# Layer one's mixing takes its block product P2 as seven inner products, placed last, and the sums for them are made earlier

## The chip, the cores and the metric

The kernel runs on one core of one Trainium2 chip. The metric is the device time of one execution in microseconds. Engines: PE (matmuls, with its weight loads PEld), DVE (vector), ACT (scalar), POOL (GpSimd) and SP, which here only issues DMAs. Each engine works through its own instructions in the order in which the program lists them. An instruction that waits holds up all that stand behind it on its engine, and the same holds for the DMAs that one queue issues.

The code counts layers from 0: `L == 0` is the first pair of blocks, which the title's "layer one" means. From here on it is called **layer zero**, and the second pair **layer one**, as in the code.

## What is computed

Four residual blocks in a row on x (2048 tokens by 512 features), A B A B:

```python
def _B_ref(x, w_in, w_sp, b_sp, w_out):
    z = _gelu(jnp.einsum("bsd,df->bsf", x, w_in))
    z1 = z[..., :Fh]
    z2 = _layernorm(z[..., Fh:], axis=-1)
    g = jnp.einsum("ts,bsf->btf", w_sp, z2) + b_sp[None, :, None]
    return jnp.einsum("bsf,fd->bsd", z1 * g, w_out)
...
x = x + _A_ref(_layernorm(x, axis=-1), A_wqkv, A_wo)
x = x + _B_ref(_layernorm(x, axis=-1), B_w_in, B_w_sp, B_b_sp, B_w_out)
x = x + _A_ref(_layernorm(x, axis=-1), A_wqkv, A_wo)
x = x + _B_ref(_layernorm(x, axis=-1), B_w_in, B_w_sp, B_b_sp, B_w_out)
```

A is linear attention with 32 heads. In B, `w_in` is 512 by 1792 (Fh = 896), `w_sp` is 2048 by 2048 and mixes the tokens, `w_out` is 896 by 512. Both layers use the same weights.

## The kernel before, in words

Tokens lie in 16 tiles of 128. Every value that is multiplied is split into a high part (ACT copies it to the matmul's type, `high`, line 100) and a low part (DVE subtracts, `low`, line 103), and a product is three matmuls: high by high, high by low, low by high (`mm3`, line 113; `acc`, line 1355).

Each layer runs through four stages. *P1* is the attention's first half. *P2* (class at line 605, `run` at 915) is the **token stage**: steps s = 1 to 18, in which a tile goes through attention's second half, its layernorm, and both halves of `w_in`. It leaves z2 in the tiles `z0` to `z15`, and z1 in DRAM. *P4* (class at line 1129, `run` at 1466) is the **mixing** `w_sp @ z2`, followed by the **output stage** (16 steps `o(i)`, line 1446): z1 times g, by `w_out`, added to x.

**The mixing as seven products.** `w_sp` is taken as 2 by 2 blocks and z2 as two halves of tokens by two groups of features (H1 and H2, with H3 the 128 columns left over), so that seven block products, P1 to P7, stand for eight. Each has eight steps k. A step has 24 matmuls of 512 columns where it also does H3 (`WITH3`: six for `delta`, 18 for `beta`), else 18. The order is P4, P2, P1, P6, P7, P5, P3 (`ORDER`). Some products go on in the banks of the one before: P1 in P2's `delta` (layer zero only), P6 and P7 in P1's `beta`, P3 in P5's. After a product's last step `evac` (line 1387) adds its banks into `gb`, and units that are then complete are queued for `gates` (line 1372): one a step, z1 loaded in one step and multiplied in by POOL in the next.

**Block sums.** P6, P7, P5 and P3 take sums of blocks of `w_sp`. `Sums` (line 1008) makes them in layer zero and keeps them in DRAM for both layers: 64 additions of 128 by 512 on POOL, two to a tick (`tick`, line 1035). The ticks come with token steps 8 to 18 and mixing steps 1, 4, 7 and 8 on. A tick first stores what the last one made, and then fetches ahead.

**The inner seven.** In layer one, P2 is itself taken as seven products of half the size, `("N", d)`, d = 0 to 13, two steps for each (`nested_mm`, line 1283), 12 matmuls a step. They use two banks X and up to two banks Y. After each product's second step, `nested_mm` itself adds the banks into `gb` on DVE (lines 1313 to 1326). Their operands are built by `token_sums`, `nested_high` and `nested_low` (lines 1240 to 1281). Three of the products take blocks of `w_sp` as they are, and four take sums that `Inner` (line 1055) makes in 16 units: a DVE addition or subtraction, a high part on ACT, a low part on DVE, and stores to DRAM. Four units stand in layer zero's token stage, four in its output stage, eight in layer one's token stage.

**One step of the mixing**, g, in this order (`run`, lines 1480 to 1506): `prepare` splits the weight of step g+2 and the tile of step g+3 (line 1204); the matmuls of step g; the DMA for the weight of step g+4 (from SP, or from POOL's queue for an inner sum); a tick of `Sums`; `gates`; in P3's steps a piece of `w_out` (`wpiece`, line 1425; its parts take over the tags of z0 to z13) and, in the last one, `zsplit(0)`, which splits the first token tile for the output stage (line 1437); then `evac`:

```python
self.mm(g)
...
    if k == 7:
        self.zsplit(0)
if p != "N" and k == HT - 1:
    self.evac(p)
```

SBUF is held as 22 pages (128 by 512), six quads for weights and split tiles, and four bigs; PSUM has eight banks. A slot that is freed goes to the end of its list, and a new tile takes the first one of it, so it waits for the last reader of that slot.

Of the kernel before, what the change touches and what calls it, by code (L numbers as in the profile page):

```python
# [21 lines left out]
NF = FH // P  # L22
# [4 lines left out]
DEFER = 6  # L27

# [25 lines left out]
def mixer_kernel(ctx: ExitStack, tc: tile.TileContext, x_in, wqkv, wo_d, win1_d, win2_d, wsp_d, bsp_d, wout_d,  # L54
# [550 lines left out]
    class P2:  # L605
# [309 lines left out]
        def run(self, sums):  # L915
            w1 = self.win1
            for s in range(1, NT + 3):
# [28 lines left out]
                else:  # L946
# [51 lines left out]
                if s == 7:  # L998
                    sums.fetch()
                if s > 7:  # L1000
                    sums.tick()
# [6 lines left out]
    class Sums:  # L1008
# [3 lines left out]
        def __init__(self):  # L1012
            self.s = {(m, k): dram.tile([P, 2, 512], F32, name=f"s{m}_{k}") for m in range(1, 5) for k in range(HT)}
            self.todo = deque((k, j, h) for k in range(HT) for j in range(2) for h in range(2))
            self.ahead = deque(self.todo)
            self.raw, self.made, self.done = {}, [], []

        def fetch(self):
            if self.ahead:
                k, j, h = self.ahead.popleft()  # L1020
                at = ((j, k), (j, k + HT), (2 + j, k)) if h == 0 else ((2 + j, k + HT),)
                self.raw.setdefault((k, j), []).extend(load(wsp_d[n, s]) for n, s in at)

        def store(self):

            for m, k, j, t in self.made:
                nc.sync.dma_start(self.s[m, k][:, j, :], t)
            pages.put(*self.done)
            self.made, self.done = [], []

        def add(self, m, k, j, t, a, b):
            nc.gpsimd.tensor_tensor(t, a, b, op=OP.add)  # L1032
            self.made.append((m, k, j, t))

        def tick(self):
            self.store()
            if not self.todo:
                return
            if not self.raw:
                self.fetch()  # L1040
            self.fetch()
            k, j, h = self.todo.popleft()
            if h == 0:
                a21, a22, a11 = self.raw[k, j][:3]
                self.add(1, k, j, a22, a21, a22)
                self.add(3, k, j, a21, a21, a11)
                self.done = [a21]
            else:
                _, a22, a11, a12 = self.raw.pop((k, j))
                self.add(2, k, j, a11, a22, a11)  # L1050
                self.add(4, k, j, a12, a11, a12)
                self.done = [a22, a11, a12]


    class Inner:
# [3 lines left out]
        def __init__(self):  # L1059
# [3 lines left out]
            self.raw, self.open, self.parts = {}, None, []  # L1063

# [8 lines left out]
        def out(self):  # L1073
            for m, k, n, p in self.parts:
                nc.sync.dma_start(self.d[m][k // 2][:, k % 2, n, :], p.bitcast(F32))
                pages.put(p)
            self.parts = []

        def finish(self, late=False):
# [5 lines left out]
            l = pages.get(PAGE, F32R)  # L1085
# [8 lines left out]
        def unit(self, late=False):  # L1094
# [20 lines left out]
            h = pages.get(PAGE, F32R)  # L1115
# [6 lines left out]
        def begin(self, n):  # L1122

            self.fetch()
            self.fetch()
            self.due, self.left = 4 * n, 4 * n - 2


    class P4:
# [3 lines left out]
        ORDER = ("P4", "P2", "P1", "P6", "P7", "P5", "P3")  # L1133
        WITH3 = ("P4", "P2", "P1", "P5")
# [6 lines left out]
        def __init__(self, p2, sums):  # L1141
# [3 lines left out]
            self.nested = p2.seven  # L1145
            self.steps = []
            for p in self.ORDER:
                if p == "P2" and self.nested:
# [7 lines left out]
            self.wout = {}  # L1156

        def fetch(self, g):
# [12 lines left out]
            elif p in ("P1", "P2", "P4"):  # L1171
                n, s = {"P1": (2, k), "P2": (2, k + HT), "P4": (0, k + HT)}[p]
# [5 lines left out]
        def operand(self, g):  # L1178
# [4 lines left out]
            if p == "P2":  # L1183
                return b[:, 0:512], 1.0, None
# [98 lines left out]
        def nested_mm(self, g):  # L1283
# [24 lines left out]
            V, bs = nc.vector, self.bs  # L1308
            for i in range(2):
                u = {n: [self.unit(2, i), self.unit(2, 2 + i), self.unit(3, i), self.unit(3, 2 + i)][n - 1]  # L1310
                     for n in range(1, 5)}
                if name == "P1":
                    V.tensor_add(u[1], self.X[i], bs[2])
# [4 lines left out]
                elif name == "P7":  # L1318
                    V.tensor_add(u[4], self.X[i], bs[3])
# [268 lines left out]
```

## Time and profile before

| | |
|---|---|
| three timed runs | 1383.07, 1383.12, 1383.37 us (median 1383.12) |
| the profiled execution | 1383.13 us |
| its span, first to last instruction | 1381.4 us |
| granted PE clock | 1.00 in the whole span |
| layer zero: mixing, output stage | 350.0 to 622.0, 622.0 to 698.2 us |
| layer one: mixing, output stage | 1034.7 to 1301.2, 1301.2 to 1377 us |
| layer one: the inner seven | 1078.2 to 1116.3 us |
| HBM | 173.87 MB read, 80.48 MB written |

Rows of groups give line, engine, operation, what it writes and reads, count, busy time, mean ns of one, and idle time ahead with what ended it. Rows of a timeline give start, duration, engine, line, and in brackets the idle time ahead and what ended it. Rows of windows give, for each stretch, its length, then the busy time (count) of PE, PEld, DVE, ACT and POOL, the PE clock, the share of time that the DMA engines are busy, and GB/s. A matmul's duration runs from its start to the modelled end of its way through the array; the next one starts earlier.

### The profile page before, as it was taken

How to read it: one execution, taken by the hardware profiler on the slowest of the kernel's cores; microseconds unless marked ns; L12 is line 12 of the kernel's file. 1: busy time of each engine (PE TensorE's matmuls, PEld its weight loads, DVE VectorE, ACT ScalarE, POOL GpSimd, SP SyncE). 2: the span in 40 equal slices, each digit the busy share in tenths (PEclk: the TensorE clock that was granted, in tenths of full speed). 3: DMA queues.
4: the chain of work that ended last, by engine and by line, in shares of the span. 5: the costliest groups of instructions: out<-in, count | busy, mean ns of one | idle time of the engine just before them, and what ended most of it. 6: DMA issues, size and time to landing. Idle time of an engine off the chain costs nothing.

```text
span 1381.4 us, 17855 instructions
## 1 busy us (share of the span) xinstructions
PE 1374.9 (100%) x6209; PEld 1153.7 (84%) x6209; DVE 942.2 (68%) x1383; ACT 603.9 (44%) x944; POOL 444.1 (32%) x521
## 2 busy tenths in 40 slices
PE   9999999999999999999999999999999999999998
PEld 7888888888888888888888888888888888888887
DVE  7776887754755487677667768877768555775642
ACT  6674544334433234233357655544454432342410
POOL 3343454544145451432113434533220101133310
PEclk9999999999999999999999999999999999999999
DMA  5542367777768974466944414677365744444442
GB/s 176 169 130 62 115 191 229 252 232 257 243 234 293 284 246 131 144 228 219 354 128 153 137 54 130 207 228 248 128 203 177 267 154 133 169 134 155 168 147 91
DMA packets 158523, 255.54 MB, mean 185 GB/s; under 512 B 13408, under 2 KB 57312, under 8 KB 157408
## 3 DMA queue, kind: packets, MB, share of 16 engines
q1 hardware_dynamic: 153680, 239.59, 53.5%
q0 software_dynamic: 2880, 11.54, 2.6%
q10 hardware_dynamic: 1872, 3.28, 0.6%
q8 instruction: 48, 0.79, 0.2%
q14 instruction: 43, 0.35, 0.1%
HBM read 173.87 MB, written 80.48 MB: 184 GB/s over the span
## 4 chain that ended last, share of the span: by engine, by line
PE 100%; DVE 0%; ACT 0%; issue 0%; DVEq 0%
PE bank L117 19%; PE bank L116 19%; PE bank L115 19%; PE bank L1359 12%; PE bank L1357 12%; PE bank L1358 12%; PE bank L1302 1%; PE bank L1299 1%; PE bank L1301 1%; PE bank L830 1%; PE bank L829 1%; PE bank L828 1%; PE bank L253 1%; PE bank L441 0%; PE bank L472 0%; ACT pg L101 0%
## 5 line engine op out<-in xcount | busy, mean ns | idle before, releaser
L1359 PE MATMUL bank<-qd,pg 128*128 128x512 f32 x736 | 286.6, 389 | 0.0
L1357 PE MATMUL bank<-qd,pg 128*128 128x512 f32 x736 | 286.6, 389 | 0.0
L1358 PE MATMUL bank<-qd,pg 128*128 128x512 f32 x736 | 286.6, 389 | 0.0
L1223 DVE TENSOR_TENSOR qd<-qd,qd 128x1024 fp32r<-128x1024 f32 x110 | 152.1, 1383 | 122.0 <-ACT qd L1213 121.4
L1213 ACT ACTIVATE qd<-qd 128x1024 fp32r<-128x1024 f32 x110 | 116.5, 1059 | 230.9 <-DMA qd<-s 110.3
L1358 PEld LDWEIGHTS bank<-qd,pg 128*128 128x128 f32 x736 | 138.2, 188 | 28.9
L1359 PEld LDWEIGHTS bank<-qd,pg 128*128 128x128 f32 x736 | 138.2, 188 | 28.5
L1357 PEld LDWEIGHTS bank<-qd,pg 128*128 128x128 f32 x736 | 138.2, 188 | 28.5
L1379 POOL TENSOR_TENSOR bg<-bg,pg 128x512 f32<-128x512 f32 x56 | 82.5, 1477 | 236.1 <-DMA pg<-z 221.3
L117 PE MATMUL bank<-qd,pg 128*128 128x512 f32 x380 | 148.5, 391 | 0.0
L230 POOL TENSOR_SCALAR rs<-mv 128x1 f32<-128x1 f32 x95 | 40.0, 422 | 317.2 <-DVE mv L228 312.6
L1032 POOL TENSOR_TENSOR pg<-pg,pg 128x512 f32<-128x512 f32 x64 | 91.2, 1425 | 92.2 <-DMA pg<-in_wsp_dram 83.8
L241 ACT ACTIVATE pg<-pg,nb,rs 128x512 f32<-128x512 f32 x63 | 51.1, 811 | 149.1 <-POOL nb L235 136.6
L115 PE MATMUL bank<-qd,pg 128*128 128x512 f32 x284 | 110.8, 390 | 0.0
L116 PE MATMUL bank<-qd,pg 128*128 128x512 f32 x284 | 110.7, 390 | 0.0
L101 ACT ACTIVATE pg<-pg 128x512 fp32r<-128x512 f32 (+1 forms) x111 | 68.0, 617 | 91.4 <-DVE pg L292 40.7
L115 PE MATMUL bank<-bg,qd 128*128 128x448 f32 x256 | 94.1, 368 | 0.0
L116 PE MATMUL bank<-bg,qd 128*128 128x448 f32 x256 | 93.7, 366 | 0.0
L117 PE MATMUL bank<-bg,qd 128*128 128x448 f32 x256 | 93.5, 365 | 0.0
L104 DVE TENSOR_TENSOR pg<-pg,pg 128x512 fp32r<-128x512 f32 (+1 forms) x109 | 80.8, 744 | 14.2 <-ACT pg L101 13.6
L292 DVE STREAM_TRANSPOSE pg<-pg 128x512 f32<-128x512 f32 x79 | 85.3, 1080 | 5.1 <-DMA pg<-xt 2.4
L116 PE MATMUL bank<-wo,qd 128*128 128x512 f32 x224 | 87.2, 389 | 0.0
(186 smaller groups left out, 2845.5 us busy)
## 6 DMA issues: line engine op xcount, KB each, us to landing
qd<-s SPq DMA_DIRECT2D x64, 512.0 KB, 3.4
qd<-in_wsp_dram SPq DMA_DIRECT2D x46, 512.0 KB, 4.8
pg<-in_wsp_dram SPq DMA_DIRECT2D x80, 256.0 KB, 4.9
s<-pg SPq DMA_DIRECT2D x64, 256.0 KB, 5.2
pg<-x SPq DMA_DIRECT2D x64, 256.0 KB, 3.5
pg<-z SPq DMA_DIRECT2D x56, 256.0 KB, 3.7
x<-pg SPq DMA_DIRECT2D x48, 256.0 KB, 3.0
z<-pg SPq DMA_DIRECT2D x44, 256.0 KB, 2.6
```

Source lines behind the costliest of these rows:

```text
L104: nc.vector.tensor_sub(l, src, h.bitcast(F32))
L115: nc.tensor.matmul(out, ah, bh, start=start, stop=False)
L116: nc.tensor.matmul(out, ah, bl, start=False, stop=False)
L117: nc.tensor.matmul(out, al, bh, start=False, stop=stop)
L292: nc.vector.transpose(y.rearrange("p c (t m) -> p m c t", m=4), r.rearrange("p (m c j) -> p m c j", m=4, c=4))
L1032: nc.gpsimd.tensor_tensor(t, a, b, op=OP.add)
L1213: nc.scalar.activation(wh, r, AF.Copy)
L1223: nc.vector.tensor_sub(wl, r, wh.bitcast(F32))
L1357: m(out, h[:, o], w[:, 0, j, :], start=start, stop=False, skip_group_check=True)
L1358: m(out, h[:, o], w[:, 1, j, :], start=False, stop=False, skip_group_check=True)
L1359: m(out, l[:, o], w[:, 0, j, :], start=False, stop=stop, skip_group_check=True)
L1379: nc.gpsimd.tensor_tensor(u, u, z1, op=OP.mult)
```

## The change

- In **both** layers P2 is now taken as the inner seven. In layer zero they stand last: P4, P1, P6, P7, P5, P3, then 14 inner steps (g = 48 to 61). Layer one keeps P4, the inner seven, P1, P6, P7, P5, P3.
- P1 always has its own `delta` and `beta`. In layer zero it adds the bias and leaves its units ungated; the inner products add into these units in place (`bs = u`), and their eight gates are queued behind the last inner step, so they fall into the output stage.
- The pieces of `w_out` go, in layer zero, to steps 49, 50, 51, 52, 55, 57 and 58. `zsplit(0)` stays in the last step, g = 61, after the step's matmuls, and therefore after the additions which `nested_mm` issues.
- `Inner` makes all 16 units in layer zero: eight in token steps 13 to 18, eight in mixing steps 11, 15, 18, 20, 25, 31, 36 and 40 (the parts of the last ones in the tags of z0 to z3). Layer one's token stage and layer zero's output stage have none.
- `Sums` makes three sums of a block in one tick, at token steps 5, 6, 8, 9, 11, 12, 14, 17 and mixing steps 1, 4, 7, 8, 10, 12, 14, 16; the fourth sums follow in 16 more ticks, at mixing steps 20 to 41, and load the second sum again from DRAM.

```diff
+TOKEN_TICKS = (5, 6, 8, 9, 11, 12, 14, 17)
+MIX_TICKS = (1, 4, 7, 8, 10, 12, 14, 16, 20, 21, 23, 24, 26, 27, 29, 30, 32, 34, 35, 37, 38, 39, 40, 41)
+MIX_UNITS = (11, 15, 18, 20, 25, 31, 36, 40)
...
-                        if (7 <= s < 14) if self.seven else (15 <= s < 18):
+                        if not self.seven and 14 <= s < 18:
                             inner.unit()
...
-                    if s == 6:
-                        inner.begin(2)
-                    elif s in (10, 11):
-                        inner.unit()
-                elif s == 14:
-                    inner.begin(1)
-                elif s in (16, 18):
+                elif s == 12:
+                    inner.begin(2)
+                elif s == 13 or 15 <= s:
                     inner.unit()
...
+                if fourth:
+                    self.raw.append((load(self.s[2, k][:, j, :]), load(wsp_d[2 + j, k + HT])))
+                else:
+                    self.raw.append([load(wsp_d[n, s]) for n, s in ((j, k), (j, k + HT), (2 + j, k))])
...
-        ORDER = ("P4", "P2", "P1", "P6", "P7", "P5", "P3")
-        WITH3 = ("P4", "P2", "P1", "P5")
+        ORDERS = ("P4", "P1", "P6", "P7", "P5", "P3", "P2"), ("P4", "P2", "P1", "P6", "P7", "P5", "P3")
+        WITH3 = ("P4", "P1", "P5")
...
-                if p == "P2" and self.nested:
+                if p == "P2":
                     self.steps += [("N", d) for d in range(14)]
...
+            self.wsteps = (49, 50, 51, 52, 55, 57, 58) if self.nest_late else range(54, 61)
...
+                bs = {n: u[n] if self.nest_late else self.bs[2 + (n > 2)] for n in u}
                 if name == "P1":
-                    V.tensor_add(u[1], self.X[i], bs[2])
+                    V.tensor_add(u[1], self.X[i], bs[1])
...
+            if name == "P5" and self.nest_late:
+                self.ready.extend((n, f, False) for n in (2, 3) for f in range(4))
...
+            sums_at = self.steps.index(("N", 0)) - (5 if self.nest_late else 4)
...
                 self.fetch(g + 4)
-                if g in (1, 4, 7) or 8 <= g < 28:
-                    self.sums.tick()
+                if self.nest_late:
+                    self.sums.tick(g, MIX_TICKS)
+                    if g == MIX_UNITS[0] - 2:
+                        inner.begin(2, 0)
+                    if g + 2 in MIX_UNITS:
+                        inner.fetch()
+                    if g == 34:
+                        inner.free = deque(range(8))
+                    if g in MIX_UNITS:
+                        inner.unit(True)
+                    elif MIX_UNITS[0] < g < 48:
+                        inner.finish(True)
...
                 self.gates()
-                if p == "P3":
-                    if k < NF:
-                        self.wpiece(k)
-                    if k == 6:
-                        self.loadx(0)
-                        self.loadx(1)
-                    if k == 7:
-                        self.zsplit(0)
+                if g in self.wsteps:
+                    self.wpiece(self.wsteps.index(g))
+                if g == n - 2:
+                    self.loadx(0)
+                    self.loadx(1)
+                if g == n - 1:
+                    self.zsplit(0)
                 if p != "N" and k == HT - 1:
                     self.evac(p)
-                if not self.nested and g == 54:
-                    inner.begin(1)
...
                 if make is not None:
-                    if i < 6:
-                        inner.unit(True)
                     make.step(i)
```

More of the change, by code (lines that the diff above doesn't have):

```diff
@@ L997, in run @@
                 w1.fetch()
[L998 to L1001, printed above, removed]
+                if not self.seven:
+                    sums.tick(s, TOKEN_TICKS)
                 if s >= NT + 1 and not self.seven:
@@ L1035, in tick @@
-        def tick(self):
+            self.made.append((m, k, j, t, done))
+        def tick(self, i, at):
             self.store()
-            if not self.todo:
+            if i + 1 in at:
+                self.fetch()
+            if i not in at:
                 return
[L1039 to L1044, printed above, removed]
+            k, j, fourth = self.todo.popleft()
+            if fourth:
+                s2, a12 = self.raw.popleft()
+                self.add(4, k, j, a12, s2, a12, s2)
+            else:
+                a21, a22, a11 = self.raw.popleft()
@@ L1063, in __init__, with part @@
             self.raw, self.open, self.parts = {}, None, []
+            self.due = 0
+            self.free = None
+        def part(self):
+            if self.free is None:
+                return pages.get(PAGE, F32R)
+            i = self.free.popleft()
+            self.free.append(i)
+            return ztag(i, PAGE, "part", F32R)
         def fetch(self):
@@ L1084, in finish @@
             m, k, h, t, keep = self.open
-            l = pages.get(PAGE, F32R)
+            l = self.part()
             low(l, t, h)
@@ L1114, in unit @@
                 pages.put(self.S2)
-            h = pages.get(PAGE, F32R)
+            h = self.part()
             high(h, t)
@@ L1345, in mm @@
                 for j in range(2):
-                    self.acc(self.delta[j], h, l, self.H3, w, j, first and (p != "P1" or self.nested),
-                             last and p != "P2")
+                    self.acc(self.delta[j], h, l, self.H3, w, j, first, last)
             for j in range(2):
```

72 lines of the change are left out of this document (31 added, 41 removed).

## The prediction, on record before the changed kernel ran

> **What bounds the kernel now.** I read the busy times first, then the chain that ended last, then the waits of the matmul engine.
>
> ```profile
> span 1381.4 us, 17855 instructions
> PE 1374.9 (100%) x6209; PEld 1153.7 (84%) x6209; DVE 942.2 (68%) x1383; ACT 603.9 (44%) x944; POOL 444.1 (32%) x521
> PE 100%; DVE 0%; ACT 0%; issue 0%; DVEq 0%
> ...
> PE bank L441 <- DVE pg L436: 2.4, 1, 2.4
> PE bank L472 <- ACT pg L101: 0.2, 1, 0.2
> ```
>
> Matmuls fill the span, the chain is PE from end to end, and PE waits twice in all, both in the first 8 us. After that no other engine ends a wait of PE anywhere. So the time falls only by matmuls taken out, and rises only by waits that come new. The profiled execution took 1383.13 us, its span is 1381.4 (1.7 lie around it), and the median of the three timed runs is 1383.12: sums made on the span carry over to the median.
>
> A matmul's price is not its mean duration, since neighbours overlap. The timeline inside layer zero's mixing, first and last of 55 matmuls in a row:
>
> ```profile
> 499.62 0.39 PE L1357 MATMUL bank<-qd,pg 128*128 128x512 f32 x1
> ...
> 511.86 0.39 PE L1357 MATMUL bank<-qd,pg 128*128 128x512 f32 x1
> ...
> L1357 PE MATMUL bank<-qd,pg 128*128 128x512 f32 x400 | 155.8, 389 | 0.0
> ```
>
> Each record lasts 0.39 us, but 54 starts lie 12.24 us apart: **0.2267 us** a matmul. The last row counts line 1357 in layer zero's mixing; lines 1358 and 1359 have as many, so that mixing has 1200 matmuls of 512 columns, 272 us.
>
> **What goes.** Product P2 of layer zero is 8 steps of 24 matmuls (delta and beta for two j), 192. Seven inner products are 14 steps of 12, 168. P1 keeps its 24 a step, in banks of its own. 24 matmuls go, 24 x 0.2267 = **-5.44 us**. Layer one already takes P2 this way, and its PE order stays.
>
> The Trainium skill, "TensorE: Matmul & The Clock Gate", section "Back-to-back issue gap", gives about 131 ns for a 512-column matmul in a sustained stream; 24 of those would be 3.1 us, not 5.4. The rows above disagree, and they are the same form in the same place, so they decide, and the 131 ns get no chance below.
>
> **What comes: the seven products placed last.** Layer zero's order becomes P4, P1, P6, P7, P5, P3, then the inner products, then the output stage, whose first matmuls need the split of the first token tile (zsplit). Today the handover from P3 looks so on DVE and PE:
>
> ```profile
> 615.88 2.17 DVE L104 TENSOR_TENSOR qd<-bg,qd 128x896 fp32r<-128x896 f32 x1
> 618.82 4.09 DVE L1419 TENSOR_TENSOR bg<-bg,bank 128x512 f32<-128x512 f32 x6 [0.77 <-PE bank L1359]
> 622.83 1.09 DVE L104 TENSOR_TENSOR qd<-bg,qd 128x896 fp32r<-128x896 f32 x1
> 621.80 0.39 PE L1359 MATMUL bank<-qd,pg 128*128 128x512 f32 x1
> 622.02 0.39 PE L115 MATMUL bank<-wo,qd 128*128 128x512 f32 x1
> 622.25 0.39 PE L116 MATMUL bank<-wo,qd 128*128 128x512 f32 x1
> 622.48 0.39 PE L117 MATMUL bank<-wo,qd 128*128 128x512 f32 x1
> ```
>
> The low half of zsplit(0) (615.88, done 618.06) stands on DVE ahead of P3's six adds out of PSUM, because the run loop calls zsplit(0) before evac. So it is ready 4 us before L117, its first reader and the third matmul of the output stage. The inner products add out of their banks inside nested_mm, which the loop calls *before* zsplit(0). In the changed order on DVE the last four adds (product P5, two per bank) stand first, then zsplit(0)'s low half, and the third output matmul still waits for it. Those adds wait for the very last matmuls of the mixing. How fast such an add follows its matmul shows in layer one's inner products, and what PE loses when it resumes on DVE shows at the start:
>
> ```profile
> 1082.04 0.39 PE L1302 MATMUL bank<-qd,pg 128*128 128x512 f32 x1
> 1082.46 0.69 DVE L1313 TENSOR_TENSOR bg<-bank,pg 128x512 f32<-128x512 f32 x1 [0.77 <-PE bank L1302]
> 1115.72 0.68 DVE L1325 TENSOR_TENSOR bg<-bg,bank 128x512 f32<-128x512 f32 x1
> 1116.32 0.68 DVE L1326 TENSOR_TENSOR bg<-bg,bank 128x512 f32<-128x512 f32 x1
> 11.29 0.69 DVE L104 TENSOR_TENSOR pg<-bank,pg 128x512 fp32r<-128x512 f32 x1 [0.45 <-ACT pg L101]
> 12.04 0.50 PE L117 MATMUL bank<-qd,pg 128*128 128x512 f32 x1
> 12.38 0.39 PE L115 MATMUL bank<-qd,pg 128*128 128x512 f32 x1
> ```
>
> An add starts 0.42 after the start of its bank's closing matmul; adds follow each other at 0.60. PE's L117 starts 0.06 after DVE's end at 11.98, and the next one comes 0.34 instead of 0.23 later: 0.17 lost on resuming. Let T be the time at which the output stage could start. The closing matmul starts at T-0.23, so the adds of the second bank start at T+0.20 and T+0.80 (those of the first are through by then), the low half at T+1.4, and it lasts 1.09: T+2.5. PE wants it at T+0.45. New wait: 2.5 - 0.45 + 0.17 = 2.2; with 0.68 between adds, as P3's six show (4.09 for six), 2.3. I take **+2.3 us**. Behind zsplit(0) on DVE stands zsplit(1)'s low half, about T+3.5, wanted by the second output step some 4.8 us (21 matmuls) after T: no second wait.
>
> **Sum:** -5.44 + 2.3 = -3.1: span 1378.3, time 1383.1 - 3.1 = **1380.0**.
>
> **What lies beside other work, and its cover.** DVE within layer zero's new inner products is the part with least cover. Layer one's, with the same tiles, and the load that is added:
>
> ```profile
> 1078.18:1116.26 38.08, 38.08 (x169) 31.55 (x168) 26.62 (x43) 15.88 (x28) 3.17 (x6) 1.00 0.71 258
> 1100.75 1.22 DVE L1223 TENSOR_TENSOR qd<-qd,qd 128x1024 fp32r<-128x1024 f32 x1
> 1103.10 1.23 DVE L1223 TENSOR_TENSOR qd<-qd,qd 128x1024 fp32r<-128x1024 f32 x1 [0.53 <-ACT qd L1213]
> L104 DVE TENSOR_TENSOR wo<-pg,wo 128x512 fp32r<-128x512 f32 x7 | 5.8, 845 | 7.5 <-ACT wo L101 7.5
> 615.40 1.71 POOL L1379 TENSOR_TENSOR bg<-bg,pg 128x512 f32<-128x512 f32 x1 [2.33 <-DVE wo L104]
> ```
>
> There DVE is busy 26.6 of 38.1 us, and the low halves of weight steps 10 and 11 end 3.4 and 3.8 us before their matmuls (1078.18 + 10 x 2.72 = 1105.38 against 1101.97). In layer zero seven wout pieces (5.8) stand between these instructions, with six gate multiplies on POOL. The pair of rows 615.40 and 615.88 prices a multiply: zsplit's low half took 2.17 under it and 1.09 without, 1.1 lost. Off go what layer one prepares there for its P1. Listing DVE in its new order at these prices, the tightest is the sixth inner step: its low half waits behind two wout pieces, the second of which is loaded into a page freed only by the second step (4.1 us to land), and comes some 12.3 us after P3's end against 13.8 needed. 1.5 us to spare; I cost it at 0, with 0 to 2 as ends. The same multiplies could hold up zsplit(0); their z1 pages come free several steps earlier, so both should be over: 0, at most 1.1.
>
> The other moves, each with the work that hides it:
>
> ```profile
> 170.00:200.00 30.00, 30.00 (x145) 26.41 (x144) 27.27 (x50) 12.62 (x21) 18.64 (x31) 1.00 0.58 180
> 513.20:545.90 32.70, 32.70 (x146) 27.07 (x145) 22.27 (x31) 13.40 (x20) 2.59 (x2) 1.00 0.40 129
> 545.90:589.40 43.50, 43.50 (x194) 36.03 (x193) 32.41 (x30) 14.10 (x21) 18.20 (x11) 1.00 0.39 134
> 182.75 1.30 POOL L109 TENSOR_TENSOR bg<-pg,bg 128x512 fp32r<-128x512 f32 x1
> 186.66 0.56 POOL L230 TENSOR_SCALAR rs<-mv 128x1 f32<-128x1 f32 x1 [2.61 <-DVE mv L228]
> ```
>
> Sums: still 64 adds of 1.3 to 1.4 us on POOL, now three to a tick from token step 5, and the fourth sums, with 16 reloads of 256 KB, in steps 20 to 41. Queued behind the first three (3.9 us into a gap of 2.6) is L230, the statistics of the next tile, 1.3 late; that tile's matmuls (e) come two token steps later: 0. Inner sums: all 16 units now in layer zero (eight in token steps 13 to 18, eight in the mixing), 0.69 twice on DVE and 0.6 on ACT each. P7 (513 to 546) gets two units and five adds, at most 2.8 + 5.5 on 22.3 of 32.7; P5 (546 to 589) one unit and six adds, at most 8 on 32.4 of 43.5. Both fit, and weights are fetched four steps ahead. SP's stores of sums wait for POOL one step later, in front of the next weight fetch, as today. What leaves layer one's token stage and layer zero's output stage saves 0, since PE waits for nothing there. Eight late gates run on POOL in output steps 1 to 8; the third chunk's four are over at step 4 and its first split comes at step 6, the last chunk's at 8 and 10: 0.
>
> **The rivals.**
> *The inner products outrun DVE* (above): +0.4 to 2 more, 1380.4 to 1382. Against it the 1.5 to spare, for it how many locks and landings that rests on.
> *zsplit(0) meets a multiply:* +1.1, 1381.1.
> *The pause cools the clock.* At the start the same matmuls come slower:
>
> ```profile
> 2.38 4.21 PE L441 MATMUL bank<-pg,ones 128*128 128x512 f32 x9 [2.38 <-DVE pg L436]
> ```
>
> Nine in 4.21 is 0.43 to 0.47 each, about twice 0.2267; four us of that cost 2: 1382. The Trainium skill, same page, table "Why this matters for your kernels", sets the limit at idle gaps of about 3 us; a pause of 2.3 stays below, and no run here shows one.
> *Slower: DMA cannot feed the inner products.*
>
> ```profile
> qd<-n POOLq DMA_DIRECT2D x8, 1024.0 KB, 5.7
> 1090.00:1095.00 5.00, 5.00 (x24) 4.14 (x23) 3.61 (x8) 0.00 (x0) 0.05 (x1) 1.00 1.06 393
> ```
>
> From the last two steps of P3 to the sixth inner step (24.5 us) six inner sums of 1 MB, two weights of 0.5 MB, and twelve z1 and wout pieces of 0.25 MB are asked for: 10.5 MB, 428 GB/s. Each sum is fetched four steps (10.9 us) ahead and lands in 5.7, 5.2 to spare; so it decides at 10.5 MB in 29.7 us, 353 GB/s. At 393, the best 5 us, nothing is late. At layer one's mean of 258 it takes 40.7 us, 11 past the spare: 1391.
> *The pause does not come* (the adds drain earlier than listed): 1377.7, the full 5.4.
>
> **Chances.** Forecast 1380.0 (1379.5 to 1380.5) 0.53; DVE outrun 0.20; multiply 0.06; clock 0.05; DMA, slower, 0.08; no pause 0.08. Measurement can tell 0.2%, 2.8 us: below 1380.35 is faster. Most of the forecast (0.46) and the no-pause case give faster 0.54; the rest of the forecast and the three middle cases same 0.38; slower 0.08. The range leaves out no-pause and DMA: **1379.0 to 1382.4**.
>
> **What would show it.** In the profile after: 24 matmuls fewer; the inner products of layer zero in 38.1 us with no wait; one new wait of PE of some 2 us, at the third matmul of layer zero's output stage, for DVE's low half of zsplit; that row beginning after four adds and lasting 1.09. Wrong if PE waits at the inner products, if the spacing after the pause is not 0.23, or if a wait stands in the token stage.

## The result, and the profile after

The changed kernel takes **1388.72 us** (median of 5 runs, 1388.44 to 1390.97) against 1383.27 of the kernel before in the same rounds: ratio 1.0043 [1.0029, 1.0058]. It is slower, by 5.5 us; the forecast was 1380.0, 3.3 faster, and its range ended at 1382.4. The profiled execution took 1388.6, its span is 1386.9, so 5.5 more than the span before.

The page of the changed kernel (span, busy times, chain by engine), then the waits of PE. Line numbers have moved by ten or so: L444 is the old L441, L107 is `low`, L104 `high`, L118 to L120 are `mm3`, L1308, L1310 and L1311 the inner matmuls.

```profile
span 1386.9 us, 17954 instructions
PE 1374.0 (99%) x6185; PEld 1151.2 (83%) x6185; DVE 967.8 (70%) x1419; ACT 606.0 (44%) x954; POOL 445.8 (32%) x529
PE 57%; DVE 0%; issue 0%; DMA 0%; SPq 0%; ACT 0%; DVEq 0%
```

```profile
PE bank L1308 <- ACT qd L1222: 4.9, 1, 4.9
PE bank L444 <- DVE pg L439: 2.4, 1, 2.4
PE bank L120 <- DVE qd L107: 1.9, 1, 1.9
```

24 matmuls fewer, as meant. But the chain, all PE before, now leaves it, and two waits are new (the 2.4 at the start is the old one): 4.9 us inside the inner products and 1.9 at the third output matmul. The first, in PE's timeline of the changed kernel (start, duration):

```profile
583.69 0.39 PE L1311 MATMUL bank<-qd,pg 128*128 128x512 f32 x1
589.01 0.77 PE L1308 MATMUL bank<-qd,pg 128*128 128x512 f32 x1 [4.93 <-ACT qd L1222]
589.58 0.63 PE L1310 MATMUL bank<-qd,pg 128*128 128x512 f32 x1
590.00 0.63 PE L1311 MATMUL bank<-qd,pg 128*128 128x512 f32 x1
```

The inner products begin at 578.48, so this is the third of their 14 steps (d = 2), asked for at 583.92. Afterwards matmuls start 0.42 apart, not 0.23. The second wait:

```profile
624.28 0.39 PE L119 MATMUL bank<-wo,qd 128*128 128x512 f32 x1
626.60 0.50 PE L120 MATMUL bank<-wo,qd 128*128 128x512 f32 x1 [1.93 <-DVE qd L107]
```

From 628.16 on matmuls start 0.43 apart here too. The granted clock explains it. Windows of the changed kernel, cut where the granted clock changes (length, busy time and count of PE, PEld, DVE, ACT, POOL; clock; DMA share; GB/s):

```profile
583.62:587.03 3.41, 0.46 (x3) 0.03 (x1) 3.38 (x7) 0.00 (x0) 2.13 (x3) 1.00 1.04 375
587.03:590.44 3.41, 1.43 (x4) 1.17 (x5) 3.41 (x5) 2.71 (x5) 0.99 (x1) 0.50 0.91 351
590.44:593.86 3.42, 3.42 (x10) 2.65 (x9) 3.42 (x6) 1.58 (x2) 0.00 (x0) 0.50 0.31 81
624.58:627.99 3.41, 1.48 (x7) 1.18 (x7) 2.96 (x4) 0.63 (x1) 0.00 (x0) 1.00 0.00 0
627.99:631.40 3.41, 3.41 (x10) 2.63 (x9) 0.00 (x0) 0.00 (x0) 0.00 (x0) 0.50 0.00 0
```

The clock changes in steps of 3.41 us, and each of these stretches in which PE was busy for 1.5 us or less is followed by one at half speed.

**The sum.** First pause 5.32 - 0.23 = 5.1, resuming 0.3, ten matmuls at half speed 2.0; handover 2.32 - 0.23 = 2.1, resuming 0.1, eight matmuls 1.6: together 11.2. Less the 5.44 that left: +5.8, where the spans differ by 5.5. No other stage has changed its length by more than 0.4 (that much shorter is the end of the kernel, behind the last output matmul).

**Who was late.** The profile names ACT for the first pause. ACT's weight split had only just ended (588.85), but it was the split for step d = 4; the third step takes an inner sum, which comes from DRAM already split. Something on DVE had just ended as well. DVE's timeline of the changed kernel, ahead of the pause and through it:

```profile
544.14 3.66 DVE L1425 TENSOR_TENSOR bg<-bg,bank 128x512 f32<-128x512 f32 x6
...
562.68 2.32 DVE L1232 TENSOR_TENSOR qd<-qd,qd 128x1024 fp32r<-128x1024 f32 x1
...
574.90 0.41 DVE L1254 TENSOR_TENSOR pg<-z_z,z_z 128x256 f32<-128x256 f32 x1
575.35 2.99 DVE L1255 TENSOR_TENSOR pg<-pg,z_z 128x256 f32<-128x256 f32 x1
578.26 1.21 DVE L1232 TENSOR_TENSOR qd<-qd,qd 128x1024 fp32r<-128x1024 f32 x1
...
580.79 3.67 DVE L1428 TENSOR_TENSOR bg<-bg,bank 128x512 f32<-128x512 f32 x6
584.37 1.40 DVE L107 TENSOR_TENSOR pg<-pg,pg 128x512 fp32r<-128x512 f32 x1
...
586.48 1.82 DVE L107 TENSOR_TENSOR pg<-z_z,pg 128x256 fp32r<-128x256 f32 x2
588.23 1.27 DVE L1323 TENSOR_TENSOR bg<-bank,bg 128x512 f32<-128x512 f32 x2
```

Before, P3's six adds (now L1428) started 3.2 us ahead of the end of the mixing (618.82 against 622.02); by that measure they are due at 575.3 and come at 580.8, **5.5 late**. Behind them stand the two adds of the first inner product out of the banks X (L1323). The third step needs them, because the inner product P6 goes on in these banks: the first add ends at 588.91 (588.23 + 0.68), and PE goes on 0.1 later. The stretched rows (2.99, 1.40, 1.82) lie beside multiplies of the gates:

```profile
575.50 2.55 POOL L1389 TENSOR_TENSOR bg<-bg,pg 128x512 f32<-128x512 f32 x2
583.96 1.26 POOL L1389 TENSOR_TENSOR bg<-bg,pg 128x512 f32<-128x512 f32 x1 [5.92 <-DVE bg L1428]
...
586.70 1.32 POOL L1389 TENSOR_TENSOR bg<-bg,pg 128x512 f32<-128x512 f32 x1 [0.94 <-DVE pg L1286]
```

An addition of 256 columns (a subtraction of that size took 0.41 in the row ahead of it) took 2.99 and ended 0.3 after the second of two multiplies. The Trainium skill, "SBUF — State Buffer", section "Who interferes with whom", says that a DVE instruction with two SBUF inputs contends with a GpSimd instruction that reads SBUF, and that such contention is an exclusive lock; the rows agree, and here two multiplies in a row held DVE for both.

The stages ahead, P7, P5 and P3 (windows of the changed kernel):

```profile
469.60:502.30 32.70, 32.70 (x146) 27.07 (x145) 28.08 (x34) 14.62 (x22) 8.25 (x6) 1.00 0.93 307
502.30:545.80 43.50, 43.50 (x193) 36.04 (x192) 40.20 (x31) 14.73 (x22) 30.86 (x18) 1.00 0.83 268
545.80:578.50 32.70, 32.70 (x146) 27.05 (x145) 29.14 (x31) 11.43 (x18) 16.82 (x12) 1.00 0.86 280
```

DVE is at 40.2 of 43.5 in P5, and the DMA engines are at 0.93 in P7 and 0.83 in P5, where they were at 0.40 and 0.39. Most of the lateness came later, though. P5's six adds, in the first DVE row above, were due at 545.8 - 3.2 = 542.6 and came 1.5 late. The other 4 us came within P3's stage, whose busy sum is only 29.1 of 32.7. There DVE was held up beside the eight multiplies of P5's gates and two of the fourth additions: four of its eight weight splits (L1232) lasted 1.94 to 2.32, such as the one at 562.68, and the other four 1.21 to 1.23. For 3.4 us it stood waiting for ACT.

### The profile page after: what moved, and what is told of

The parts are those of the page before. It is cut to its first block, busy times and chain, and to the rows that moved or that the text cites. A ratio compares the mean times of both kernels' runs of the same rounds, so it can differ in the third digit from the quotient of the medians.

```text
span 1386.9 us, 17954 instructions
## 1 busy us (share of the span) xinstructions
PE 1374.0 (99%) x6185; PEld 1151.2 (83%) x6185; DVE 967.8 (70%) x1419; ACT 606.0 (44%) x954; POOL 445.8 (32%) x529
## 4 chain that ended last, share of the span: by engine, by line
PE 57%; DVE 0%; issue 0%; DMA 0%; SPq 0%; ACT 0%; DVEq 0%
PE bank L120 11%; PE bank L119 11%; PE bank L118 11%; PE bank L1368 5%; PE bank L1367 5%; PE bank L1369 5%; PE bank L1308 2%; PE bank L1310 2%; PE bank L1311 2%; PE bank L833 1%; PE bank L832 1%; PE bank L831 1%; DMA pg<-in_wout_dram 0%; PE bank L256 0%; DVE qd L1232 0%
## 5 line engine op out<-in xcount | busy, mean ns | idle before, releaser
L1367 PE MATMUL bank<-qd,pg 128*128 128x512 f32 x672 | 261.4, 389 | 0.0
L1368 PE MATMUL bank<-qd,pg 128*128 128x512 f32 x672 | 261.4, 389 | 0.0
L1369 PE MATMUL bank<-qd,pg 128*128 128x512 f32 x672 | 261.4, 389 | 0.0
L1232 DVE TENSOR_TENSOR qd<-qd,qd 128x1024 fp32r<-128x1024 f32 x108 | 156.1, 1446 | 91.5 <-ACT qd L1222 91.0
L120 PE MATMUL bank<-qd,pg 128*128 128x512 f32 x380 | 148.3, 390 | 0.0
L1367 PEld LDWEIGHTS bank<-qd,pg 128*128 128x128 f32 x672 | 126.1, 188 | 26.3
L1369 PEld LDWEIGHTS bank<-qd,pg 128*128 128x128 f32 x672 | 126.1, 188 | 26.3
L1368 PEld LDWEIGHTS bank<-qd,pg 128*128 128x128 f32 x672 | 126.1, 188 | 26.0
L1033 POOL TENSOR_TENSOR pg<-pg,pg 128x512 f32<-128x512 f32 x64 | 95.6, 1494 | 135.4 <-DMA pg<-in_wsp_dram 96.4
L104 ACT ACTIVATE pg<-pg 128x512 fp32r<-128x512 f32 (+1 forms) x117 | 72.0, 618 | 124.5 <-DVE pg L295 42.7
L118 PE MATMUL bank<-qd,pg 128*128 128x512 f32 x284 | 110.7, 390 | 0.0
L119 PE MATMUL bank<-qd,pg 128*128 128x512 f32 x284 | 110.6, 389 | 0.0
L107 DVE TENSOR_TENSOR pg<-pg,pg 128x512 fp32r<-128x512 f32 (+1 forms) x115 | 86.3, 753 | 22.3 <-ACT pg L104 18.3
L118 PE MATMUL bank<-bg,qd 128*128 128x448 f32 x256 | 94.0, 367 | 0.0
L120 PE MATMUL bank<-bg,qd 128*128 128x448 f32 x256 | 93.4, 365 | 0.0
L120 PE MATMUL bank<-wo,qd 128*128 128x512 f32 x224 | 88.0, 393 | 1.9 <-DVE qd L107 1.9
```

The costliest lines, as they stand in the source:

```text
L107: nc.vector.tensor_sub(l, src, h.bitcast(F32))
L118: nc.tensor.matmul(out, ah, bh, start=start, stop=False)
L119: nc.tensor.matmul(out, ah, bl, start=False, stop=False)
L120: nc.tensor.matmul(out, al, bh, start=False, stop=stop)
L1232: nc.vector.tensor_sub(wl, r, wh.bitcast(F32))
L1367: m(out, h[:, o], w[:, 0, j, :], start=start, stop=False, skip_group_check=True)
```

## The experiments

Ratios are to the kernel before, timed on the same chip in the same rounds (1383.16 to 1383.33). "Gap" means the distance of two matmul starts; 0.23 of it is no loss.

**1. zsplit(0) ahead of the last inner step's matmuls** (layer zero).

```diff
+                if self.nest_late and g == n - 1:
+                    self.zsplit(0)
                 self.mm(g)
...
-                if g == n - 1:
+                if not self.nest_late and g == n - 1:
                     self.zsplit(0)
```

> The changed kernel with zsplit(0) of layer zero issued before the matmuls of the last inner step, so ahead of their four adds on DVE. If the pause at the third output matmul (2.3 us between starts, then eight matmuls at 0.43) comes from the low half standing behind these adds, that pause and its slow matmuls go, 2.2 + 1.6 = 3.8 us: 1384.9. Rival: the pause has another cause (the split's page or ACT's high half): it stays, 1388.7. The wait at the third inner step stays in both.

1384.07 (1382.27 to 1388.12, 10 runs), ratio 1.0009 [1.0000, 1.0018]: 4.7 less than the change. The output stage of this kernel starts without a pause:

```profile
623.38 0.39 PE L119 MATMUL bank<-wo,qd 128*128 128x512 f32 x1
623.61 0.39 PE L120 MATMUL bank<-wo,qd 128*128 128x512 f32 x1
```

So the handover's cause is the one that was predicted, and it was expected to give 3.8. The rest of the 4.7 lies elsewhere: the first pause is shorter here (gap 3.14), and a new one stands at inner step 10 (gaps 1.07 and 1.26). P5's adds were on time in this kernel (542.58), and P3's came 4.0 late (579.25), although nothing ahead of them differs from the change.

**2. The pieces of w_out later:** the first four by four steps, the last three by one or two. Theory A: DVE's add out of bank X ends the first pause. Theory B: ACT does, since a piece of w_out that had not landed stood ahead of the weight split.

```diff
-            self.wsteps = (49, 50, 51, 52, 55, 57, 58) if self.nest_late else range(54, 61)
+            self.wsteps = (53, 54, 55, 56, 57, 58, 59) if self.nest_late else range(54, 61)
```

> The changed kernel with the first wout pieces four steps later (steps 53 to 59 instead of 49 to 58). Theory A (DVE reaches P3's adds 5.5 us late, and the add that frees bank X0 for the third inner step stands behind them): the wait of 5 us at the third inner step stays within 1 us, 1388 to 1389. Theory B (ACT stands waiting for a wout piece to land, 7.6 us, with the weight's high half behind it, as the inferred releaser says): the wait goes with its slow matmuls, some 7.4 us, 1381 to 1382.

1387.46 (1383.41 to 1389.25), ratio 1.0028 [1.0019, 1.0038]. The pause stays (gap 4.95): theory B falls for this pause. The median is just below the 1388 to 1389 of theory A; P3's adds are 5.2 late.

**3. No fourth sums.** Their 16 additions and 32 loads are left out, and product P3 takes the second sums instead.

```diff
-MIX_TICKS = (1, 4, 7, 8, 10, 12, 14, 16, 20, 21, 23, 24, 26, 27, 29, 30, 32, 34, 35, 37, 38, 39, 40, 41)
+MIX_TICKS = (1, 4, 7, 8, 10, 12, 14, 16)
...
-            self.todo = deque([(k, j, False) for k, j in at] + [(k, j, True) for k, j in at])
+            self.todo = deque((k, j, False) for k, j in at)
...
+                if m == 2:
+                    nc.sync.dma_start(self.s[4, k][:, j, :], t)
```

> The changed kernel without the 16 additions of the fourth sums and without their 32 loads; the fourth sum's place in DRAM gets the second sum instead, so P3 computes another product. If DVE's lateness at P3's adds comes from the fourth sums (POOL's adds holding up DVE, and their loads), DVE reaches these adds on time and the wait at the third inner step goes: 1381 to 1382, the pause at the output stage left. Rival (the late DVE comes from the inner units and the gates, as before): the wait stays above 3 us, 1387 to 1389.

1386.21 (1383.49 to 1387.42), ratio 1.0019 [1.0009, 1.0028]. The first pause is gone from the profile (P3's adds start at 575.66, on time), but 2.5 us is less than the 7 expected: gaps of 0.67, 0.47, 2.31 and 1.26 come at inner steps 7 to 10, and the handover keeps its 2.31. A second wait was hidden behind the first. The profiled execution took 1384.0, 2.2 below the median; whether the first pause is gone from the others isn't known.

**4. P3's adds two inner steps later**, behind the adds that PE waits for.

```diff
-                if p != "N" and k == HT - 1:
+                if p == "P3" and self.nest_late:
+                    pass
+                elif p != "N" and k == HT - 1:
                     self.evac(p)
+                if self.nest_late and g == 49:
+                    self.evac("P3")
```

> The changed kernel with P3's six adds (evac) issued two inner steps later, behind the adds of the first inner product. Theory A: the add that frees X0 no longer stands behind six others (3.7 us), so the wait at the third inner step falls from 5 to 1.5 us or less; with fewer slow matmuls 1383 to 1385. Theory B (ACT behind a wout piece): the wait stays at 5 us, 1388 to 1389.

1385.83 (1384.48 to 1387.18), ratio 1.0018 [1.0009, 1.0028]. The first pause goes with the adds out of the way: theory A holds. Smaller gaps come at steps 4 and 6 (0.83, 0.78), and larger ones at step 10 (2.69, 1.26, 0.59). The 2.69 ends when ACT has split that step's weight, at 609.05; a piece of w_out, which ACT could only take up at 607.47 when it had landed, stood ahead of it.

**5 and 6. Both edits, then with P3's gates held back** until inner step 8. The sixth adds to edits 1 and 4:

```diff
-                self.gates()
+                if not (self.nest_late and 48 <= g < 56):
+                    self.gates()
```

> The two edits of before together, nothing left out: zsplit(0) ahead of the last inner step's matmuls, and P3's six adds issued two inner steps later. If the three pauses (second inner step, tenth inner step, handover) have causes of their own, the two edits add up: no handover pause (2.1 us off the 1385.8 that the second edit gave alone), no pause at the second inner step, and the 4 us at the tenth stay: 1383.0 to 1384.0. Rival, pauses shift into one another: whatever is taken away early comes back at the tenth step, which then grows above 5 us: 1385 to 1386.

> As the run with both edits, and P3's six gates (z1 loads on SP's queue, multiplies on POOL) are held back until inner step 8, so that the weights of inner steps 10 and 11 are asked for ahead of them. Theory: the tenth step pauses because its weight's DMA stands behind z1 loads on SP that wait for pages; then the pause of some 4 us goes and nothing is left of the three: 1378.0 to 1380.0. Rival, DVE is simply behind at the tenth step (six locks and seven pieces of w_out): the pause shrinks by no more than the multiplies' locks, 1 to 2 us: 1381.5 to 1383.

Both edits: 1383.59 (1382.49 to 1386.89), 1.0006 [0.9996, 1.0015]. With held gates: **1379.93** (1379.01 to 1382.28), 0.9979 [0.9969, 0.9989]. Both medians fell where the theories had them, but the profiles show another place. With both edits the gaps are 1.62 at inner step 4, 2.60 at step 6 and 1.04 at step 10, where some 4 us were expected; with held gates 0.82, none and 1.23. So step 10's did not shrink from the one to the other. What went is mainly the pause at step 6, with the stretch at half clock behind it, and its cause was a lock. DVE with both edits, then POOL:

```profile
593.45 4.05 DVE L1288 TENSOR_TENSOR pg<-z_z 128x256 f32<-128x256 f32 x2
597.42 1.27 DVE L1325 TENSOR_TENSOR bg<-bank,bg 128x512 f32<-128x512 f32 x2
```

```profile
593.74 1.31 POOL L1389 TENSOR_TENSOR bg<-bg,pg 128x512 f32<-128x512 f32 x1
...
595.59 1.28 POOL L1389 TENSOR_TENSOR bg<-bg,pg 128x512 f32<-128x512 f32 x1
```

DVE with held gates:

```profile
593.09 0.76 DVE L1288 TENSOR_TENSOR pg<-z_z 128x256 f32<-128x256 f32 x2
```

Two subtractions took 4.05 beside two of the gates' multiplies, and 0.76 without them. The add out of the bank that step 6 goes on in stood behind them, and PE went on at 598.20.

The DMA issues of SP changed too, first with both edits only:

```profile
592.14 0.37 SPq L100 DMA_DIRECT2D pg<-in_wout_dram  x1
599.32 0.33 SPq L100 DMA_DIRECT2D pg<-z  x1
599.70 0.43 SPq L1181 DMA_DIRECT2D qd<-in_wsp_dram  x1
```

and with held gates:

```profile
592.94 3.10 SPq L1181 DMA_DIRECT2D qd<-in_wsp_dram  x2
```

The weights of inner steps 10 and 11 (L1181) stood behind a z1 load that waited 7 us for a page; without it they are asked for 6.8 us earlier, and the next piece of w_out 4.8 earlier. The high half of step 10's weight is ready at 605.50 instead of 610.56. PE comes to step 10 at 606.3 with held gates, so at 610.56 it would have stood there for some 4 us (worked out from these rows, not run); with both edits alone it came only at 610.8, because it had stood at steps 4 and 6. That such a wait for the weight goes when the gates are held is seen between the fourth kernel (gap 2.69 at step 10) and the ninth, which only adds the held gates to it (none; a gap of 1.09 for the low half is left). So the queue and the locks both count, and how the 3.7 us divide between them isn't shown.

**7 and 8. The fourth sums in two halves.** Seven leaves the 16 additions out and keeps the loads; eight keeps 16 additions (of other operands) and leaves the loads out.

```diff
-                self.add(4, k, j, a12, s2, a12, s2)
+                self.made.append((4, k, j, a12, (s2,)))
```
```diff
-                    self.raw.append((load(self.s[2, k][:, j, :]), load(wsp_d[2 + j, k + HT])))
+                    self.raw.append((pages.get(PAGE), pages.get(PAGE)))
...
-                self.add(4, k, j, a12, s2, a12, s2)
+                self.add(4, k, j, a12, self.b[0], self.b[1], s2)
...
+                    self.sums.b = self.bs
```

> The change with the 16 fourth additions on POOL left out; their 32 loads and 16 stores stay (the fourth sum is then a block of w_sp as it is). It tells apart what in the fourth sums makes DVE late for the second inner step. Theory POOL (an addition on POOL stretches a DVE operation that runs beside it from 1.2 to 2.3 us): the pause at the second inner step is gone, as when both were left out, 1384 to 1386. Rival DMA (the loads' 8 MB hold back the weights that ACT and DVE then split late): the pause stays, 4 to 5 us, 1387 to 1389.

> The counterpart: the 16 fourth additions stay on POOL (of two bias tiles that lie there), their 32 loads of 256 KB are left out, the 16 stores stay. Theory POOL: the pause at the second inner step stays, 4 to 5 us: 1387 to 1389. Rival DMA: it goes, 1384 to 1386. If it goes in neither or in both of the two, the two act together and the excess of each is under the 5.5 us that DVE was late.

1386.45 (1383.77 to 1389.72), 1.0024 [1.0014, 1.0034], and 1386.56 (1382.27 to 1389.00), 1.0021 [1.0012, 1.0031]. In the two profiles P3's adds start at 578.85 both times, 4.0 and 3.3 late, and the first pause stays, with gaps of 4.47 and 2.30. It goes in neither, which had been set down as the case in which additions and loads act together. That they do isn't shown: the first kernel, with both of them, was 4.0 late as well, and in time leaving out either (2.3 and 2.2) was worth as much as leaving out both (2.5), with spreads of 6 us in these two.

The seventh kernel tells where the lateness arises. DVE is busy for only 26.7 of 43.2 us in its P5, and P5's adds are on time to the hundredth (P5 ends at 545.38):

```profile
542.18 4.16 DVE L1425 TENSOR_TENSOR bg<-bg,bank 128x512 f32<-128x512 f32 x6
```

One stage later P3's adds are 4.0 late. So P3's stage makes DVE late by itself.

**9. Only the handover left**: edits 4 and 6 without edit 1.

> The change with P3's adds issued two inner steps later and P3's gates held back until inner step 8, but zsplit(0) left where the change puts it; nothing is left out. Only the predicted pause is left, at the third matmul of the output stage: 2.31 between starts, 2.1 lost. Theory: it adds its 2.1 to the 1379.9 that the same kernel gives without it, 1382.0, and, where it falls whole into one window of 3.41 us of the clock, another 1.7 for a window at half clock (in some of the runs, so that these lie at 1382 and at 1383.7 with a granted clock of 1.000 and 0.999). Rival: the pause is hidden by the slack that the kernel wins elsewhere (below 1381), or it costs its 2.1 and no clock in any run (all within 0.8 of 1382).

1383.22 (1381.02 to 1384.19, 11 runs), 0.9998 [0.9989, 1.0006]: 3.3 more than the same kernel with zsplit(0) first. The pause costs its 2.1, and in some runs the clock as well. The profiled one is such a run:

```profile
619.51:622.92 3.41, 1.36 (x6) 0.83 (x5) 3.33 (x5) 0.95 (x1) 1.28 (x1) 1.00 0.00 0
622.92:626.34 3.42, 3.42 (x10) 2.68 (x9) 0.22 (x1) 0.00 (x0) 0.00 (x0) 0.50 0.00 0
```

Four of the eleven runs show a mean clock below 1.000 and lie at 1383.1 to 1384.2; the other seven lie at 1381.0 to 1383.5. The first are slower by about 1 us on average, but the two groups that I expected do not separate, and a mean of 0.999 also stands in runs of the kernel before, which has no such pause.

**10 and 11. The last three pieces of w_out moved** to inner steps 9, 10 and 11, behind the weight splits on ACT; both on top of edits 1, 4 and 6. In ten the gates were also held longer, to step 10, in eleven to step 8 as before.

```diff
-            self.wsteps = (49, 50, 51, 52, 55, 57, 58) if self.nest_late else range(54, 61)
+            self.wsteps = (49, 50, 51, 52, 57, 58, 59) if self.nest_late else range(54, 61)
```

> All edits together, nothing left out: zsplit(0) first, P3's adds two inner steps later, its gates held until inner step 10, and the three late pieces of w_out moved to inner steps 9, 10 and 11, behind the split of the weights of steps 10 and 11 on ACT. Theory: of the two small pauses that were left with both edits and held gates (0.82 and 1.23 between starts), the second goes, since a piece of w_out that has not landed stood ahead of the weight's high half on ACT: 1 us less, 1378.5 to 1379.5. Rival: ACT's order does not matter there, DVE is the one behind: 1379.5 to 1380.5, the pause stays or shifts to a later inner step.

> As the kernel with all edits that paused 5.75 us in the output stage because the last gate's z1 came too late, but with the gates held only until inner step 8, as in the run at 1379.9; the three late pieces of w_out stay at inner steps 9, 10 and 11. Nothing is left out. Theory: neither pause comes; what is left is the one of 0.8 at the third inner step: 1378.2 to 1379.6. Rival: with z1 loads and pieces both behind inner step 8 again, the pieces land late for the output stage or their multiplies hold up DVE at the last inner steps: a pause at inner step 11 or later, 1379.8 to 1382.

Ten: 1387.10 (1386.14 to 1388.12), 1.0028 [1.0017, 1.0038]; a miss. The gap at inner step 10 is gone, but the output stage has one of 5.75. Its POOL and SP rows:

```profile
678.42 1.26 POOL L1389 TENSOR_TENSOR bg<-bg,pg 128x512 f32<-128x512 f32 x1 [5.58 <-DMA pg<-z]
```

```profile
669.96 2.54 SPq L100 DMA_DIRECT2D pg<-in_wqkv_dram  x4
...
673.02 1.48 SPq L100 DMA_DIRECT2D pg<-z  x1
```

The z1 of one of the last gates is asked for behind the next layer's weights, and POOL idles 5.6 us until it has landed. Eleven, with two steps less of delay: **1378.75** (1378.35 to 1379.31), 0.9967 [0.9954, 0.9979], the lowest median of all, though its interval overlaps those of the sixth and the twelfth; one gap is left (0.83, inner step 4, for a low half on DVE). There the weight of step 10 is split on ACT at once, where in the sixth kernel it stood behind a piece that had to land, as these rows show, the sixth first and the eleventh then:

```profile
603.92 0.63 ACT L104 ACTIVATE wo<-pg 128x512 fp32r<-128x512 f32 x1 [8.95 <-DMA pg<-in_wout_dram]
604.46 1.04 ACT L1222 ACTIVATE qd<-qd 128x1024 fp32r<-128x1024 f32 x1
```

```profile
602.20 1.06 ACT L1222 ACTIVATE qd<-qd 128x1024 fp32r<-128x1024 f32 x1 [6.84 <-DMA qd<-in_wsp_dram]
```

**12. P3's adds left where the change has them**: edits 1 and 6 alone.

> zsplit(0) first and the gates held, but P3's adds left where the change issues them; nothing is left out. With the runs that leave out one of the other two edits it tells what each is needed for. Theory: P3's six adds still stand ahead of the low half and the adds that the second inner step waits for, and holding the gates only takes one lock of 1.1 us away: a pause of some 2 us stays at the second inner step, 1381.5 to 1383.5. Rival: the locks alone made DVE late, and with the gates held the place of the six adds does not matter: 1379.5 to 1380.5.

**1379.76** (1377.71 to 1380.97), 0.9975 [0.9965, 0.9984]. The rival holds: with the gates held no difference from the place of the six adds can be measured. DVE of this kernel:

```profile
578.11 3.67 DVE L1428 TENSOR_TENSOR bg<-bg,bank 128x512 f32<-128x512 f32 x6
...
583.77 1.28 DVE L1323 TENSOR_TENSOR bg<-bank,bg 128x512 f32<-128x512 f32 x2
...
617.11 1.89 DVE L107 TENSOR_TENSOR qd<-bg,qd 128x896 fp32r<-128x896 f32 x1
```

The adds are still 2.8 late, but nothing behind them is stretched, and PE loses 0.6 there. It loses another 1.3 at the handover (gap 1.53): zsplit(0)'s low half, 1.07 in the sixth kernel, took 1.89 beside a multiply that began at 616.77. That is the rival which the prediction called a meeting of zsplit(0) and a multiply.

Side by side, in us:

| zsplit(0) first | P3's adds later | gates held | pieces later | median |
|---|---|---|---|---|
| | | | | 1388.72 (the change) |
| x | | | | 1384.07 |
| | x | | | 1385.83 |
| x | x | | | 1383.59 |
| | x | x | | 1383.22 |
| x | | x | | 1379.76 |
| x | x | x | | 1379.93 |
| x | x | x | x | 1378.75 |

Putting zsplit(0) first is worth 4.7 on the change and 3.3 with the gates held; holding the gates 4.3 with zsplit(0) first and 2.6 with the later adds. The later adds are worth 2.9 alone, 0.5 with zsplit(0) first and nothing beside held gates. Differences of a microsecond or so lie within the intervals, which reach 1.2 to 2 us either way. Holding the gates alone wasn't tried.

## Why the prediction was wrong

- **-5.44 for 24 matmuls: right.** The kernel with all four edits has one pause left, 0.6 us and 0.1 on resuming, and its profiled span is 1376.6, 4.8 less than before.
- **Handover +2.3 at the third output matmul: right**, in place, cause and size, but for the clock below. PE lost 2.1 there and 0.1 on resuming, and the low half began right behind the four adds; with zsplit(0) first (run 1) the pause was gone:

```profile
624.86 0.68 DVE L1336 TENSOR_TENSOR bg<-bg,bank 128x512 f32<-128x512 f32 x1
625.46 2.08 DVE L107 TENSOR_TENSOR qd<-bg,qd 128x896 fp32r<-128x896 f32 x2
```

- **DVE within the inner products at 0, "1.5 us to spare", ends 0 to 2: the step that failed.** The list began "after P3's end" with a DVE that is on time there. It was 5.5 us late, and so PE waited at the third step (5.1, and 2.3 more for resuming and clock), not at the sixth, which I had called the tightest. P3's six adds and the stretched operations around them stood ahead of the add that frees the third step's bank; with the six adds out of the way (run 4) this pause was gone. As a rival it had 0.20, priced at +0.4 to 2.
- **"Both fit", of P7 and P5: the sums right, P3's stage missing.** For P5 I had 32.4 + 8 = 40.4 of 43.5, and 40.2 came. P5 left DVE 1.5 us late; the other 4 came in P3's stage, for which I had made no sum. The token sums and the first inner operands are new there, and the eight multiplies of P5's gates run there, each of which can stretch what DVE does beside it. Its busy sum, 29.1 of 32.7, looks as if it fitted, too: the 3.4 us that DVE waited for ACT don't count in it, and P3's adds are due before the stage ends. DMA's share, which I did not add up for P7 and P5, went from 0.4 to 0.8 and 0.9.
- **A multiply meets zsplit(0): did not come there** (two low halves in 2.08), but the same lock stretched three operations ahead of the third step. In the twelfth kernel it came, at 1.3 us.
- **DMA cannot feed the inner products, 1391, given 0.08: the nearest time, with half of the mechanism.** In the change no weight was late; in runs 1 to 4 and 8 PE waited for one at step 10 (gaps of 0.74 to 2.69), but through the order in SP's queue and on ACT, and not for want of bandwidth as far as the twelfth kernel tells. I put the point at 353 GB/s; that kernel moved 350 from 578.5 to 597.5, and PE lost 0.6 in the stretch.
- **The pause cools the clock, given 0.05, +2: it happened.** 1.6 at the handover, 2.0 after the first pause. I had held against it that 2.3 us is below a limit of about 3. The Trainium skill, "TensorE: Matmul & The Clock Gate", section "Part 1: The HAM clock gate (the "warmup" mystery)", describes a free-running window of about 3.4 us and an idle one as the condition; the window agrees (3.41), the condition does not: a window with 1.48 us of work in it counted as idle.
- **Token stage and sums at 0: right.** PE has no new wait there.

What stays open: why the same instructions up to P3's end leave DVE 4.0 to 5.5 us late (the first kernel, the second and the change). Locks and waits for ACT both show in the rows, and one profiled run of each kernel does not tell their shares.

## What to carry to other kernels

Add up every stage up to the point where the new work begins, with the waits and with what another engine's lock can add; here the one stage left out made 4 of the 5.5 us. Start the list of an engine's work from where it really stands when the new part begins, and walk to the first due time, not to the one that looks tightest. When a step moves, go through the order of the queue it issues on: a load that waits for a page holds up the weights behind it. Putting what can wait (here six gates, their loads and their multiplies) behind what can't was worth 2.6 to 4.3 us. Count a pause of PE together with the clock that may follow it.

## What was not expected of the hardware

Whether a pause cools PE depends on where it lies against a grid of 3.41 us. In nine kernels' profiles, twelve stretches of that grid at full clock with PE busy for 0 to 1.50 us were each followed by one at half clock (for instance 1.48 and 1.36 above); with 1.54 and more none was, and nothing lay between. The second kernel, with the later pieces of w_out, shows the same gap at its handover (624.95 to 627.26). Counted on from its last change of the clock, the grid splits it between two stretches, and it cools nothing:

```profile
623.03:626.44 3.41, 2.30 (x11) 1.57 (x9) 2.81 (x5) 1.30 (x2) 0.42 (x1) 1.00 0.00 0
626.44:629.85 3.41, 2.59 (x11) 2.18 (x12) 1.77 (x2) 0.00 (x0) 0.00 (x0) 1.00 0.00 0
```

At half clock more work was needed to get back: a stretch with 2.29 us busy was followed by another at half clock (run 10, 679.58 to 683.00), one with 2.87 by full clock (run 4, 609.81 to 613.23). A pause of 1.9 us without matmuls is thus enough if it falls whole into one stretch, and costs some 1.6 us more. Part of the spread between runs of one kernel may come from there; that isn't shown.
